# Start-up transfers reordered, two constant rows written on the chip, and two smaller expert buffers in a fused attention, gate and expert kernel

## The chip, the cores and the metric

The kernel runs on one core of a Trainium2 chip. The metric is the device time of one execution in microseconds (us); the number of record is the median of several executions. A profiled execution gives, beside its time, a trace of every instruction on the five engines: TensorE (PE, its weight loads apart as PEld), VectorE (DVE), ScalarE (ACT), GpSimd (POOL) and SyncE (SP, which here only issues transfers).

## The reference

Three layers follow each other on a batch of 2 sequences of 768 tokens. Attention has 8 heads of 64; a query sees the keys that fall to the same of 16 centroids. A gated projection of width 512 follows, and then 8 experts of 512 x 1024 x 512, of which each token uses one.

```python
q_assign = np.argmax(np.einsum('bhsd,hcd->bhsc', q_n, c_n), axis=-1)
mask = q_assign[:, :, :, None] == k_assign[:, :, None, :]
scores = np.where(mask, scale * np.matmul(q, k.transpose(0, 1, 3, 2)), -1e9)
attn = softmax(scores); x = attn @ v
...
out = sigmoid(causal_conv5(x, conv_w)) * (x @ w_val) @ w_out
...
e = fresh_e if s == 0 or local_gate[b, s] < 0.5 else prev_e
h = np.maximum(x[b, s] @ w1[e], 0.0)
out[b, s] = p[e] * (h @ w2[e])
```

## The kernel before

Heads are taken in 8 pairs. For a pair, `load` (L155) brings the transposed queries `qt` and keys `kt`, 128 x 768 floats each, through SP's queue. `assign` (L165 to L211) finds the centroid of every token: PE multiplies `qt` and `kt` with the normalised centroids `cT` into `sim` (L172), DVE transposes that (L177), takes the maximum (L182), compares (L185) and transposes back (L188), and for the first pair L201 makes the one-hot rows `rb`. Those rows stand under the 64 rows of each head in `km` (keys) and `q2` (queries): rows 0 to 63 hold the rounded values, 64 to 79 the one-hot rows, 80 to 95 zeros, and row 96 of `km` ones, so that one product gives score, mask and maximum. `cT` is made by `setup` from `cw` (the centroids) and `ident` (an identity matrix), through DVE, ACT and one transpose on PE (L133 to L143). `fixed` fills rows 80 to 96 from an array of zeros and ones, called `one`, in main memory, with transfers that POOL issues; there are three sets of `km` and `q2` for the pairs to take in turn.

The order within the first pairs is written out by hand, as tables of places (`FIRST`, `ORDER`, `GO`, `PLAN`). An engine runs its instructions in the order in which the program issues them, and so DVE, in the first pair, transposes `sim` of the second pair (L177) ahead of making `rb` of the first (L201).

The experts are sorted by the number of their tokens. The one of rank r gets a buffer of `CAPS[r]` places, fixed when the program is built; up to 128 tokens of one expert are done ahead of the others. A token that finds no place is left to a loop at the end (`beyond`), which loads an expert's whole weights anew for a block of 128; its number of rounds is a value that the chip computes. The work on an expert is `up` (eight steps over the 512 inputs, L1408 and L1411, for buffers of 256 places or fewer) and `down` (L1447, and L1455 for a last tile of 32 or 64 tokens). In `up`, high and low part of the tokens stand side by side:

```python
nc.tensor.matmul(ps[:, m, :2 * n], lhsT=hi[:, k, ms], rhs=x[:, k, :2 * n], ...)   # L1408
nc.tensor.matmul(ps[:, m, :256], lhsT=lo[:, k, ms], rhs=x[:, k, :256], ...)       # L1411
```

with n the number of places: 2n columns in the first. In `down`, each full tile of 128 tokens, or of 96, takes three products of 512 columns for each of eight rows of weights (L1447). A last tile of 64 or 32 tokens takes plain 32-bit products in groups side by side instead (L1455), 256 columns wide for 64 tokens and 128 wide for 32:

```python
def rest(self, r):
    return m if (m := self.cap(r) % 128) in (32, 64) else 0
```

ACT and DVE round the weights (L1353, L1354) four to five steps ahead of PE.

Of the kernel before, what the change touches and what calls it, by code (L numbers as in the profile page):

```python
# [31 lines left out]
N = B * S  # L32


CAPS = [320, 288, 256, 224, 192, 192, 160, 128]
NC = 3
NBLK = 12
KEEP = -1.7881393e-07
# [1 line left out]
def tiles(n):  # L40
    return -(-n // 128)


def f32(ap):
    return ap.bitcast(F32)


class Attn:
# [41 lines left out]
    def consts(self):  # L90

        nc, g, cp, tp = self.nc, self.g, self.cp, self.tp
        self.cw = cp.tile([128, 128], F32, name="cw")
        nc.sync.dma_start(self.cw, g["cw"])
        nc.sync.dma_start(self.ident, g["ident"])
        self.before = cp.tile([128, 128], BF16, name="before")
        nc.gpsimd.dma_start(self.before, g["before"])

        self.oq = [cp.tile([128, S], F32R, name=f"oq{i}") for i in range(2)]
        self.eh = [cp.tile([128, 128], F32R, name=f"eh{i}") for i in range(2)]  # L100
        self.negbig = cp.tile([128, 1], F32, name="negbig")
        nc.vector.memset(self.negbig, -BIG)

    def fixed(self, i):

        nc, g = self.nc, self.g
        nc.gpsimd.dma_start(self.km[i][80:97, :, :].rearrange("o a s -> o (a s)"), g["one"])
        nc.gpsimd.dma_start(self.q2[i][80:96, :, :].rearrange("o a s -> o (a s)"), g["one"][0:16])

# [475 lines left out]
    def run(self, work, beside):  # L585

        G = B * NP
        drain = lambda it: [None for _ in it]
        self.tiles = [(gi, i, a) for gi in range(G) for i in range(0, 12, 1 if gi < 2 else 2)
                      for a in range(2 if gi < 2 else 3)]  # L590
        self.last = 0
        self.consts()
        self.step("one", 0)
        self.load(0)
        self.load(1)
        self.setup()
        self.first_pair(work)
        self.todo = [(gi, j) for gi in range(1, G) for j in range(NT)]
        for gi in range(1, G):
            self.pair(gi, work, beside)  # L600
        drain(work)
        self.pvs((G, 0))
        drain(self.sums_mm(G - 1))
        self.main.close()
# [664 lines left out]
class Ffn:  # L1269
# [16 lines left out]
    @staticmethod  # L1286
    def cap(r):
        return 128 if r < 0 else CAPS[r]

# [11 lines left out]
    def turn(self, ps, tag, pool, r, i):  # L1301

        nc, n = self.nc, self.cap(r)
        if i == 0:

            self.x[r] = pool.tile([128, KD, 2 * max(CAPS) if r >= 0 else n],
                                  F32R if r >= 0 else F32, tag="x", name=f"x{r}")
# [76 lines left out]
    def up(self, ps, pool, r, c):  # L1384
# [4 lines left out]
        if c == 0:  # L1389
            self.h[r] = [pool.tile([128, KF, max(CAPS)], F32R, tag=t, name=f"{t}{r}", bufs=1)  # L1390
                         for t in ("hh", "hl")]
# [93 lines left out]
    def run(self, wst, wp, pg, late, ctx):  # L1485
# [9 lines left out]
        def turn(r, i):  # L1495
            free = ("o2",) if tiles(CAPS[r - 1]) < 3 else ()
            spare = 0 < i <= len(free)
            self.turn(ps_o if spare else ps_t, free[i - 1] if spare else "t", p2, r, i)
# [3 lines left out]
        for s in range(8, last):  # L1502
            r, c = s // 8 - 1, s % 8
            if c == 4 and r + 2 < E:
                self.gather(pg, r + 2)
            if r + 1 < E and c >= 5 and c - 5 < tiles(CAPS[r + 1]):
                turn(r + 1, c - 5)
# [275 lines left out]
def consts():  # L1783
# [7 lines left out]
    e = np.arange(E, dtype=f)  # L1791
    cap = np.array(CAPS)
    i = np.arange(E)
# [43 lines left out]
def host_moe(inputs):  # L1837
    cc = np.ascontiguousarray
    o = {}

    o["w_val"], o["w_out"] = (cc(inputs["moe_" + n]).view(np.int64) for n in ("w_val", "w_out"))
    o["conv"] = cc(inputs["moe_conv_w"].T.reshape(KD, 128, KC).transpose(1, 0, 2)).view(np.int64)
    wgl = np.concatenate([inputs["moe2_w_gate"], inputs["moe2_w_local"]], axis=1)
    o["wgl"] = cc(wgl.reshape(KD, 128, E + 1).transpose(1, 0, 2))
    o["w1"], o["w2"] = cc(inputs["moe2_w1"]), cc(inputs["moe2_w2"])
    o["ident"] = np.eye(128, dtype=np.float32)
    o["rc"], o["tri"] = consts()
    o["jc"] = cc(np.repeat(np.arange(NBLK, dtype=np.float32)[:, None], 128, axis=1))
    return o
# [55 lines left out]
```

## Time and profile before

| | us |
|---|---|
| median of three runs (the others 560.71 and 567.31) | 566.21 |
| the profiled execution's own time | 563.89 |
| its span | 562.1 |
| PE busy | 522.1 |
| DVE busy | 387.3 |
| ACT busy | 293.8 |
| POOL busy | 257.9 |

Times in the rows are in us from the start of the span unless ns is written. A row of the timeline gives start, length, engine, line, operation, what is written and read, and in brackets how long the engine stood idle ahead of it and who ended that. PE's busy time includes the overlap of pipelined matmuls, so a busy PE isn't PE at its peak.

### The profile page before, as it was taken

What the parts mean: (1) busy time and instruction counts of PE and PEld (TensorE: products, weight loads), DVE (VectorE), ACT (ScalarE), POOL (GpSimd) and SP (SyncE); (2) the same over time, 40 slices, a digit from 0 to 9 for tenths busy, and PEclk for the clock granted to TensorE, in tenths of its full rate; (3) what the DMA queues carried; (4) which work ended last, traced back from release to release, by engine and by line L of the source; (5) the groups of instructions that cost most, each with busy time, mean ns of one, the idle gap of its engine ahead of it and who ended that gap; (6) DMA issues with size and microseconds to landing.
All of it is one profiled execution on the core that took longest, in us unless ns stands there. A gap on an engine that the chain in (4) does not pass through costs nothing. (4 is left out here: it accounts for less than half of the span.)

```text
span 562.1 us, 9334 instructions
## 1 busy us (share of the span) xinstructions
PE 522.1 (93%) x3328; PEld 387.0 (69%) x3328; DVE 387.3 (69%) x694; ACT 293.8 (52%) x569; POOL 257.9 (46%) x195
## 2 busy tenths in 40 slices
PE   3898979999998999999988999999999999999992
PEld 0564545565655665667678899859898888978892
DVE  4756768787788689767978563646737568479671
ACT  2635354554554565686464241435534548559671
POOL 4475728697897878877931010042013133022011
PEclk9998897999999999999999999999999999999997
DMA  8896284676757452200000038289364887556840
GB/s 203 216 228 184 88 219 127 172 185 169 199 153 174 120 141 81 67 12 0 1 10 0 21 108 305 94 272 342 114 205 162 281 251 232 179 182 211 295 166 14
DMA packets 53180, 86.90 MB, mean 155 GB/s; under 512 B 6313, under 2 KB 30321, under 8 KB 53132
## 3 DMA queue, kind: packets, MB, share of 16 engines
q1 hardware_dynamic: 49996, 78.36, 47.1%
q0 software_dynamic: 3136, 7.92, 4.4%
q8 instruction: 27, 0.44, 0.3%
q14 instruction: 21, 0.17, 0.1%
HBM read 59.65 MB, written 8.62 MB: 121 GB/s over the span
## 5 line engine op out<-in xcount | busy, mean ns | idle before, releaser
L307 DVE TENSOR_REDUCE mn<-mx 128x1 f32<-128x512 f32 (+1 forms) x156 | 94.3, 639 | 29.6 <-PE mx L303 29.4
L398 ACT ACTIVATE p<-s 128x384 f32<-128x384 f32 x168 | 75.4, 488 | 58.5 <-PE s L397 55.3
L1354 DVE TENSOR_TENSOR wl<-ws,wh 128x1024 fp32r<-128x1024 f32 x64 | 77.5, 1222 | 11.0 <-ACT wh L1353 9.8
L476 POOL TENSOR_TENSOR acc<-acc,p 128x768 f32<-128x768 f32 x42 | 84.4, 2033 | 0.5
L1353 ACT ACTIVATE wh<-ws 128x1024 fp32r<-128x1024 f32 x64 | 66.6, 1056 | 6.3 <-DMA ws<-in_w_dram 6.3
L396 PE MATMUL s<-xq,xk 128*128 128x384 f32 x168 | 63.9, 380 | 3.4 <-ACT p L398 3.4
L1480 POOL DMA_INDIRECT out_dram<-o,L x12 | 14.5, 1212 | 112.5 <-ACT o L1479 99.2
L492 PE MATMUL pv<-p,v 128*64 128x384 f32 x336 | 64.8, 507 | 0.0
L303 PE MATMUL mx<-km,q 80*128 80x512 f32 (+1 forms) x192 | 60.7, 387 | 2.3 <-DVE mn L307 1.9
L397 PE MATMUL s<-q,km 97*128 97x384 f32 x168 | 57.4, 342 | 0.0
L1408 PE MATMUL ph<-x,wh 128*128 128x384 f32 (+4 forms) x192 | 56.5, 338 | 0.0
L396 PEld LDWEIGHTS s<-xq,xk 128*128 128x128 f32 x168 | 32.0, 191 | 34.7 <-issue 19.2
L796 DVE SCALAR_TENSOR_TENSOR gp<-xT,cwt,gp 128x767 f32<-128x767 f32 (+3 forms) x32 | 51.5, 1625 | 2.5 <-ACT gp L790 2.1
L1411 PE MATMUL ph<-x,wl 128*128 128x256 f32 x192 | 51.6, 279 | 0.0
L303 PEld LDWEIGHTS mx<-km,q 80*128 80x128 f32 x192 | 37.3, 207 | 15.4 <-DVE mn L307 8.1
L492 PEld LDWEIGHTS pv<-p,v 128*64 128x64 f32 x336 | 20.7, 138 | 27.8 <-issue 27.4
L1447 PE MATMUL po<-wh,hh 128*128 128x512 f32 x96 | 39.0, 407 | 0.0
L1408 PEld LDWEIGHTS ph<-x,wh 128*128 128x128 f32 x192 | 36.1, 188 | 3.2 <-issue 1.0
L1447 PE MATMUL po<-wh,hl 128*128 128x512 f32 x96 | 37.8, 393 | 0.0
L1447 PE MATMUL po<-wl,hh 128*128 128x512 f32 x96 | 37.6, 391 | 0.0
L1411 PEld LDWEIGHTS ph<-x,wl 128*128 128x128 f32 x192 | 36.0, 188 | 0.1
L476 POOL TENSOR_TENSOR acc<-p,p 128x768 f32<-128x768 f32 x14 | 26.2, 1884 | 20.7 <-ACT p L398 20.7
(350 smaller groups left out, 1096.7 us busy)
## 6 DMA issues: line engine op xcount, KB each, us to landing
ws<-in_w_dram SPq DMA_DIRECT2D x72, 512.0 KB
qt<-in_qT_dram SPq DMA_DIRECT2D x8, 384.0 KB
kt<-in_kT_dram SPq DMA_DIRECT2D x8, 384.0 KB
q<-hiq SPq DMA_DIRECT2D x16, 192.0 KB
km<-hik SPq DMA_DIRECT2D x16, 192.0 KB
v<-in_v_dram SPq DMA_DIRECT2D x8, 384.0 KB
xk<-kt SPq DMA_DIRECT2D x16, 192.0 KB
xk<-hik SPq DMA_DIRECT2D x16, 192.0 KB
```

Of the source, the lines that this page charges most:

```text
L303: nc.tensor.matmul(ps[:, n * p:n * p + n], lhsT=q2[0:80, h, t * 128:t * 128 + 128], rhs=km[0:80, h, c:c + n], start=(p == 0), stop=True, s ...
L307: nc.vector.tensor_reduce(out=out, in_=src, axis=AX.X, op=ALU.max)
L396: nc.tensor.matmul(ps, lhsT=kl[:, h, ks], rhs=t1[:, h, hs], start=True, stop=False)
L397: nc.tensor.matmul(ps, lhsT=km[:97, h, ks], rhs=q2[:97, h, hs], start=False, stop=True)
L398: nc.scalar.activation(pt[:, h, hs], ps, AF.Exp, scale=1.0 / D ** 0.5)
L476: eng.tensor_tensor(t[:, h], p(0)[:, h] if first is None else t[:, h], p(j)[:, h], op=ALU.add)
L492: nc.tensor.matmul(self.pvt[64 * h:64 * h + 64, i, :HS], lhsT=v[:, j, 64 * h:64 * h + 64], rhs=pt[:, h, half(i)], start=False, stop=(j == ...
L1353: nc.scalar.activation(hi, t, AF.Copy)
L1354: nc.vector.tensor_tensor(lo, t, f32(hi), op=ALU.subtract)
L1408: nc.tensor.matmul(ps[:, m, :2 * n], lhsT=hi[:, k, ms], rhs=x[:, k, :2 * n], start=st, stop=False, skip_group_check=True)
L1411: nc.tensor.matmul(ps[:, m, :256], lhsT=lo[:, k, ms], rhs=x[:, k, :256], start=False, stop=sp, skip_group_check=True)
L1447: nc.tensor.matmul(self.po[r][i][:m], lhsT=a[:, k, ts], rhs=w[:, q], start=(k == 0 and z == 0), stop=(k == KF - 1 and z == 2))
```

## The change

There are three edits. The first pair's four transfers are issued ahead of everything else on SP, and those of `cw` and `ident` move from SP to ACT's queue. The rows of `km` and `q2` for the first pair are written by three memsets on POOL, from row 64 on, in place of two transfers of 17 and 16 rows of 1536 floats that POOL issued; the other pairs keep the transfers. The third and the sixth expert's buffers shrink from 256 to 224 and from 192 to 160 places.

```diff
-CAPS = [320, 288, 256, 224, 192, 192, 160, 128]
+CAPS = [320, 288, 224, 224, 192, 160, 160, 128]
...
-        nc.sync.dma_start(self.cw, g["cw"])
-        nc.sync.dma_start(self.ident, g["ident"])
+
+        nc.scalar.dma_start(self.cw, g["cw"])
+        nc.scalar.dma_start(self.ident, g["ident"])
...
     def fixed(self, i):
 
         nc, g = self.nc, self.g
+        if i == 0:
+
+            nc.gpsimd.memset(f32(self.km[0][64:96, :, :]), 0.0)
+            nc.gpsimd.memset(f32(self.km[0][96:97, :, :]), 1.0)
+            nc.gpsimd.memset(f32(self.q2[0][64:96, :, :]), 0.0)
+            return
...
         self.last = 0
+        self.load(0)
         self.consts()
         self.step("one", 0)
-        self.load(0)
         self.load(1)
```

The line numbers after the first edits are 7 higher. SP's queue at the start of the program, before (`qt_137`, `kt_139` are the first pair's, `qt_141`, `kt_143` the second's, `hiq` and `hik` their rounded values):

```order
L94 DMA cw<-in_cw_dram 128x128
L95 DMA ident<-in_ident_dram 128x128
L155 DMA qt_137<-in_qT_dram 128x768
L155 DMA kt_139<-in_kT_dram 128x768
L155 DMA qt_141<-in_qT_dram 128x768
L155 DMA kt_143<-in_kT_dram 128x768
L264 DMA q_0_85<-hiq_175 64x768 x2
L264 DMA km_88<-hik_194 64x768 x2
```

SP's queue at the same place with the change:

```order
L162 DMA qt_124<-in_qT_dram 128x768
L162 DMA kt_126<-in_kT_dram 128x768
L162 DMA qt_142<-in_qT_dram 128x768
L162 DMA kt_144<-in_kT_dram 128x768
L271 DMA q_0_85<-hiq_176 64x768 x2
L271 DMA km_88<-hik_195 64x768 x2
```

Two rows have left the head of SP's queue. ACT's first instructions with the change; before, they are the same without the two transfers:

```order
L95 DMA cw<-in_cw_dram 128x128
L96 DMA ident<-in_ident_dram 128x128
L142 ACT_TABLE_LOAD
L142 ACTIVATE css<-css 128x1
L268 ACTIVATE hiq_176<-qt_124 128x768
```

The two transfers stand ahead of ACT's first table load. PE at the end of the sixth expert and the start of the seventh, before (`po` are the outputs, `ws` the weights as loaded, `hr` the last tile's hidden values):

```order
L1447 MATMUL po_0_5589<-wh_5578,hl_5450 128x512
L1455 MATMUL po_1_5590<-ws_5380,hr_5476 64x256 x4
L1455 MATMUL po_1_5590<-ws_5400,hr_5476 64x256 x4
L1455 MATMUL po_1_5590<-ws_5419,hr_5476 64x256 x4
L1455 MATMUL po_1_5590<-ws_5447,hr_5476 64x256 x4
L1408 MATMUL ph_0_5672<-x_5603,wh_5597 128x320
```

PE at the same place with the change:

```order
L1454 MATMUL po_0_5590<-wh_5579,hl_5451 128x512
L1462 MATMUL po_1_5591<-ws_5381,hr_5477 32x128 x8
L1462 MATMUL po_1_5591<-ws_5401,hr_5477 32x128 x8
L1462 MATMUL po_1_5591<-ws_5420,hr_5477 32x128 x8
L1462 MATMUL po_1_5591<-ws_5448,hr_5477 32x128 x8
L1415 MATMUL ph_0_5689<-x_5604,wh_5598 128x320
```

Nothing has moved there: 16 products of 256 columns have become 32 of 128. In the same way the 32 first products of the third expert's `up` go from 512 to 448 columns and those of the sixth's from 384 to 320.

## Rows read from the trace of the kernel before

**Rows 1.** Stretches of 20 us: busy time and instructions of each engine, granted clock, transfers.

```profile
core 0: us, PE busy (x) PEld busy (x) DVE busy (x) ACT busy (x) POOL busy (x), PEclk, DMA share, GB/s
0.00:20.00 20.00, 9.01 (x57) 3.18 (x57) 10.35 (x24) 7.06 (x12) 9.59 (x19) 1.00 0.91 227
...
440.00:460.00 20.00, 20.00 (x106) 16.92 (x105) 16.86 (x27) 14.55 (x21) 6.07 (x5) 1.00 0.84 276
```

**Rows 2.** Waits from 437.8 to 552 us: sum, number, longest.

```profile
ACT hs L1416 <- PE ph L1411: 34.5, 9, 7.9
```

**Rows 3.** Stretches of single steps of four experts, the same columns as rows 1.

```profile
437.84:449.25 11.41, 11.41 (x69) 9.92 (x65) 6.76 (x12) 7.37 (x12) 1.37 (x1) 1.00 0.86 283
461.06:471.30 10.24, 10.24 (x65) 9.74 (x64) 5.90 (x8) 7.01 (x11) 1.35 (x1) 1.00 0.66 200
503.00:512.28 9.28, 9.28 (x66) 9.28 (x65) 5.07 (x8) 6.33 (x13) 1.15 (x1) 1.00 1.04 350
522.52:531.06 8.54, 8.54 (x67) 8.54 (x65) 4.53 (x7) 5.89 (x12) 1.18 (x1) 1.00 1.05 355
518.92:522.52 3.60, 3.60 (x33) 2.22 (x32) 2.50 (x4) 0.53 (x1) 0.00 (x0) 1.00 0.90 318
537.12:539.00 1.88, 1.88 (x65) 1.68 (x64) 1.88 (x3) 0.91 (x1) 0.00 (x0) 1.00 0.79 288
449.25:461.06 11.81, 11.81 (x59) 9.73 (x58) 10.09 (x16) 7.18 (x10) 4.70 (x4) 1.00 0.78 252
471.30:483.46 12.16, 12.16 (x58) 9.03 (x57) 9.02 (x11) 6.75 (x10) 3.39 (x3) 1.00 0.92 292
```

**Rows 4.** Timeline of SP at the start.

```profile
0.73 0.41 SPq L94 DMA_DIRECT2D cw<-in_cw_dram  x1
...
1.67 0.42 SPq L155 DMA_DIRECT2D qt<-in_qT_dram  x1
```

**Rows 5.** Timeline of PE at the start: first and last product with `cT`.

```profile
6.71 0.87 PE L172 MATMUL sim<-qt,cT 128*32 128x192 f32 x8 [2.00 <-DMA qt<-in_qT_dram]
...
11.84 0.87 PE L172 MATMUL sim<-kt,cT 128*32 128x192 f32 x8 [0.49 <-DMA kt<-in_kT_dram]
```

**Rows 6.** Timeline of DVE at the start.

```profile
2.63 0.29 DVE L133 TENSOR_TENSOR csq<-cw 128x128 f32<-128x128 f32 x1 [1.77 <-DMA cw<-in_cw_dram]
...
4.75 0.29 DVE L143 COPY cT<-pc 128x128 f32<-128x128 f32 x1 [0.57 <-PE pc L141]
...
9.53 0.58 DVE L177 STREAM_TRANSPOSE s<-sim 128x384 f32<-128x384 f32 x1 [4.22 <-PE sim L172]
...
11.89 0.58 DVE L188 STREAM_TRANSPOSE et<-eq 128x384 bf16<-128x384 bf16 x1
12.78 0.58 DVE L177 STREAM_TRANSPOSE s<-sim 128x384 f32<-128x384 f32 x1 [0.31 <-PE sim L172]
```

**Rows 7.** Stretch from 4 to 12 us, the same columns as rows 1.

```profile
4.00:8.00 4.00, 1.34 (x9) 0.41 (x9) 0.74 (x4) 0.84 (x1) 0.00 (x0) 1.00 1.09 294
8.00:12.00 4.00, 1.89 (x20) 0.56 (x24) 2.37 (x4) 0.84 (x1) 2.36 (x2) 1.00 1.02 242
```

**Rows 8.** Timeline of ACT at the start.

```profile
0.72 1.28 ACT L135 ACT_TABLE_LOAD   x1 [0.72 <-PEq L1894]
3.27 0.20 ACT L135 ACTIVATE css<-css 128x1 f32<-128x1 f32 x1 [1.27 <-DVE css L134]
```

**Rows 9.** Timeline of POOL at the start.

```profile
1.27 0.72 POOL L97 DMA_DIRECT2D before<-in_before_dram  x1 [0.84 <-POOLq L1894]
...
9.64 1.81 POOL L269 TENSOR_TENSOR kt<-kt,hik 128x768 f32<-128x768 f32 x1 [6.53 <-PE sim L172]
...
16.08 1.41 POOL L124 MEMSET oq<- 64x768 f32 x2
```

**Rows 10.** Stretch from 55 to 60 us, columns as rows 1; PE's idle time ahead.

```profile
55.00:60.00 5.00, 5.00 (x14) 2.48 (x12) 4.83 (x11) 1.07 (x3) 1.18 (x1) 0.50 0.42 120
52.26 0.52 PE L343 MATMUL mt<-identr,mfr 128*128 128x128 f32 x3 [2.19 <-DVE mfr L338]
```

## Prediction

> **What bounds the kernel now.** I read the stretches first. In the experts' part PE is busy for 20.00 of 20 us, while DVE, the next, is busy for 16.86 in its fullest stretch [rows 1]. PE runs its products one behind the other there, so what shortens a product shortens the end. The sum of waits says that the others are ahead: ACT stood idle nine times, 34.5 us in all, until PE had finished a step of `up` [rows 2]. The first 20 us are another matter. PE is busy for 9.01 of them and the transfers take a share of 0.91 [rows 1], so the timelines of the start have to be followed from wait to wait. The page's chain of waits doesn't help, since it ends within the last few microseconds.
>
> At the start PE begins its first product with `cT` at 6.71, when `qt` has landed, and its last at 11.84, when the second pair's `kt` has landed [rows 5]. DVE transposes the first result at 9.53 and has the first pair's one-hot form at 11.89 + 0.58 = 12.47. Then it waits 0.31 for the last `sim` and transposes it at 12.78 [rows 6]. The first pair's `rb` stands behind that on DVE, and with it the first products of the masked scores. So of the four transfers it is the last that sets the start's end; `cT`, ready at 4.75 + 0.29 = 5.04 [rows 6], doesn't.
>
> **The change part by part. The third expert.** Its `up` was 32 products of 512 columns and 32 of 256, and took 11.41 us. With 224 places it is what the fourth expert is now, 448 and 256 columns, which took 10.24 [rows 3]: 1.17 off. Its `down` keeps two tiles with three products each per row of weights, since 96 isn't 32 or 64. It took 11.81, and the fourth's, with a last tile of 96, 12.16 [rows 3]. The 0.35 between them also holds other turned tiles and starts, so the loss lies between 0 and 0.35; I take 0.2.
>
> **The sixth expert.** `up` goes from 9.28 to what the seventh shows, 8.54: 0.74 off. Its last tile goes from 64 to 32 tokens, from 3.60 to 1.88 [rows 3]: 1.72 off, the largest single term. The full tile stays. Smaller transposes, evictions and gathers are put at nothing: they lie on ACT, DVE and POOL beside PE, and if their cover went, the ACT waits [rows 2] would have to be used up first, 34.5 us over nine waits, some 3.8 each against 2.5 us that leave the sixth expert. On the path this sums to -1.17 + 0.2 - 0.74 - 1.72 = -3.43, with bounds of -3.2 and -3.7.
>
> **The transfers at the start.** `qt` is issued at 1.67 and now would be at 0.73, in the place of `cw` [rows 4]: 0.94 earlier, and the three others with it. The rows of zeros and ones leave the queues: 33 rows of 6144 bytes, 203 KB, which at the 294 and 242 GB/s of the stretch from 4 to 12 us [rows 7] are 0.7 to 0.8 us of transfer time ahead of the last `kt`. If both count in full, the last `kt` lands 1.7 earlier. But `cw` and `ident`, 64 KB each, now run among the four instead of ahead of them, and 131 KB at the same rates are 0.5 us. If they push the four back by all of that, 1.2 remains; if the transfers, full as they are [rows 7], gain by bytes alone, 0.75; and the trace doesn't show how two queues share, so a lower end of 0.3 is kept. The upper end is 2.2, if 6144 bytes into single rows cost twice their bytes' share. I take 1.4, between the two sums. The stages behind are tied to each other by waits, so a shift at the start should reach the end unchanged.
>
> DMA issue is the subject of a rule. SP's rows show that a transfer takes about 0.42 of the issuing engine [rows 4]. The Trainium skill, "DMA: Bandwidth & Descriptors", section "Issuing engines are not separate DMA queues", says that transfers run on the same 16 engines and interleave whoever issues them, and that a second issuer saves only issue time. By that rule the start's gain would be the bytes' 0.75 and the whole change 4.2 us. The stretch from 4 to 12 us, with its engines full [rows 7], agrees; the first microseconds, in which `qt` waits to be issued, don't.
>
> **ACT.** Two issues of 0.42 come ahead of its table load, which started at 0.72 and takes 1.28: it would end at about 2.9. The next instruction starts at 3.27, behind DVE [rows 8]. So this costs nothing while DVE isn't earlier, and at most 0.8 if it were; what is queued behind it, the rounding of `qt`, isn't on the path before `qt` lands.
>
> **POOL.** Its issue of `before` ends at 1.99, and the three memsets follow. None of 1536 columns is in the trace. Two of 768 columns took 1.41 [rows 9], so one of 1536 costs 1.4, and three 4.2: POOL is free at about 6.2. If partitions and columns both count against it, 3 x 2.8 puts that at 10.4. Its next work starts at 9.64 behind PE's second product [rows 9], with the change some 1.4 earlier, at 8.2. At 6.2 the memsets are hidden; at 10.4 they push POOL's subtraction of `kt` by 2.2, which only feeds a transfer for the lower scores, and those come after the first masked maxima. I take nothing. ACT's and DVE's writes of the one-hot rows now also wait for POOL, and come behind `rb`, so later than 12.
>
> **The sum.** -3.43 - 1.4 = -4.8 us. The profiled execution took 563.89, 562.1 of it the span; that less 4.8 is 559.1. The median of the three runs, 566.21, lies 2.3 above it, and the mean of the four executions is 564.5. I take that mean as the base: **560 us** rounded, 1.1% below the median.
>
> **The rivals. The start gives nothing.** Another late arrival takes the place of the last `kt`, for instance the rounded keys, whose transfers stand behind all four in SP's queue. For it: transfers are at 1.09 and 1.02 of their engines from 4 to 12 us [rows 7]. Against it: bytes leave this stretch. Only the experts' part remains: 564.5 - 3.4 = 561.
>
> **The constants come too late: slower.** `cw` was first in line and was there by 2.63; `cT` was ready 2.41 later, and from there two products of 0.87 and DVE's work from 9.53 to 12.47 lead to the transpose of the second pair [rows 5, 6]. That is 2.41 + 1.74 + 2.94 = 7.1 from `cw` to a point that stands at 12.78 now. So `cw` may land up to 5.7 and cost nothing beside today's start, and from 9.2 on it eats the experts' 3.4 too. If ACT's queue is served behind SP's, `cw` lands when the last `kt` does now, 11.84: the point moves to 18.9, 6.1 later, and the time is 564.5 + 6.1 - 3.4 = 567. For it: SP issues first and asks for 1.6 MB. Against it: POOL's `before`, issued at 1.27 on a third queue [rows 9], was in time. The same skill page, "Queues, rings and completion order", has each transfer engine take turns between queues, which would put `cw` behind about one of the four; no row here shows such turns.
>
> **A low-clock stretch goes.** From 55 to 60 us the granted clock is 0.50, the lower level of 1.2 GHz, after PE had stood idle for 2.19 us behind DVE [rows 10]. If the shift shortens that idle time and the clock stays at 2.4, up to half of these 5.0 busy us come back: 560 - 2.5 = 557. Against it: that idle time comes from DVE's order of work, which the change leaves alone.
>
> **It doesn't do what it says.** If the third expert had more than 224 tokens, or the sixth more than 160, the end's loop would run a round. From the 225th token on that costs 4.2 MB of weights, 15 us at 276 GB/s [rows 1], and two layers of products behind it; 15 more is an estimate from that: about 590. The reference's own inputs put 220 and 104 tokens there, so four places are left.
>
> **How the numbers follow.** The forecast has 0.70, no gain at the start 0.15, a low-clock stretch gone 0.08, constants too late 0.05, the extra round 0.02. Two per cent, 11.3 us, is about what a measurement of this kernel can tell from no change; the three runs lie 6.6 apart. The bounds of the terms give -3.5 to -5.9, so 558.6 to 561 around the base, and the runs' spread around their mean (-4 and +3) goes on top: **555.5 to 565**. That takes in the first three cases, and leaves out the other two and the far ends. Faster by over 2% needs less than 554.9, which takes the gone stretch and a low run: 0.05. Slower by over 2% is the extra round: 0.02. The rest, 0.93, is within 2%.
>
> **What would show it.** The first `sim` should start between 5 and 6.5, the last at about 10.4, and DVE's transpose of it at about 11.4. POOL's memsets should end by 7. `up` of the third and sixth expert should take 10.2 and 8.5, the sixth's last tile 1.9, and PE should still have no wait there. The prediction is wrong if PE waits in the sixth expert for rounded weights, if `cT` comes after 7.5, or if what the start gains is waited away before 60 us.

## The result: 1% faster, as forecast, but the start gained in another way

| | before | after |
|---|---|---|
| median of 20 runs each, us | 564.87 | 558.79 |
| lowest and highest | 560.71, 567.82 | 555.92, 564.18 |
| ratio, 95% interval | | 0.9905, 0.9883 to 0.9926 |
| span of the profiled execution | 562.1 | 558.3 |
| first product of the masked scores (`mx`) starts at | 16.11 | 14.98 |
| PE's work on the experts takes | 171.38 | 167.90 |

The forecast was 560 and no change that a measurement can tell at 2%; the ratio is 5.4 us off the time before. Ratios here leave out the runs of the slower state, over 1.5% above their kernel's fastest, and of the profiles below only that of "`cw` first, again" is from such a run. The experts first. These are stretches of the changed kernel, with the columns of [rows 1]: `up` and `down` of the third expert, `up` and the last tile of the sixth.

```profile
437.88:448.23 10.35, 10.35 (x68) 9.86 (x65) 5.92 (x12) 6.68 (x11) 1.35 (x1) 1.00 0.91 303
448.23:460.17 11.94, 11.94 (x58) 9.09 (x57) 10.32 (x17) 7.31 (x10) 4.45 (x4) 1.00 0.80 252
502.13:510.66 8.53, 8.53 (x66) 8.53 (x65) 4.53 (x7) 5.89 (x12) 1.18 (x1) 1.00 1.01 336
517.30:519.18 1.88, 1.88 (x65) 1.68 (x64) 1.88 (x4) 0.50 (x1) 0.87 (x1) 1.00 0.86 272
```

Beside [rows 3] that is 11.41 to 10.35, 11.81 to 11.94, 9.28 to 8.53 and 3.60 to 1.88: -1.06 + 0.13 - 0.75 - 1.72 = -3.40. PE is busy in all of each stretch, and ACT still waits for it, 32.4 us in eight waits where [rows 2] have 34.5 in nine:

```profile
ACT hs L1423 <- PE ph L1418: 32.4, 8, 7.8
```

The start is another matter. PE, DVE and POOL in the changed kernel, with the lines that answer to [rows 5, 6, 9] (line numbers 7 higher; the first two rows are PE's first and last product with `cT`, the third is the first `mx`):

```profile
7.24 0.87 PE L179 MATMUL sim<-qt,cT 128*32 128x192 f32 x8 [0.38 <-DVE cT L150]
...
9.16 0.87 PE L179 MATMUL sim<-kt,cT 128*32 128x192 f32 x8
...
14.98 1.01 PE L310 MATMUL mx<-km,q 80*128 80x384 f32 x2
```

```profile
4.43 0.29 DVE L140 TENSOR_TENSOR csq<-cw 128x128 f32<-128x128 f32 x1 [3.57 <-DMA cw<-in_cw_dram]
...
5.70 0.62 DVE L146 TENSOR_SCALAR cn<-cw,css 128x128 f32<-128x128 f32 x1
6.89 0.29 DVE L150 COPY cT<-pc 128x128 f32<-128x128 f32 x1 [0.56 <-PE pc L148]
8.81 0.58 DVE L184 STREAM_TRANSPOSE s<-sim 128x384 f32<-128x384 f32 x1 [1.36 <-PE sim L179]
...
11.78 0.54 DVE L184 STREAM_TRANSPOSE s<-sim 128x384 f32<-128x384 f32 x1
```

```profile
2.03 1.37 POOL L110 MEMSET km<- 32x1536 f32 x1
3.46 1.37 POOL L111 MEMSET km<- 1x1536 f32 x1
4.87 1.37 POOL L112 MEMSET q<- 32x1536 f32 x1
```

The first product now starts behind `cT`, not behind `qt`, and the last has no wait for `kt` any more. In the records of the transfers the last `kt` landed at 8.29, 3.5 earlier than the 11.80 before; the sum had allowed at most 2.2. And `cw` landed at 4.41 where it was 2.60, so `cT` was ready at 6.89 + 0.29 = 7.18 in place of 5.04. All four products ran behind it in one go, and from the first transpose at 8.81 to the second at 11.78 DVE had no gap. The transpose of the second pair went from 12.78 to 11.78 and the first `mx` from 16.11 to 14.98: 1.13 where the sum had 1.4.

### The profile page after: what moved, and what is told of

Its sections match the earlier page's. It is cut to its first block, busy times and chain, and to the rows that moved or that the text cites. A ratio compares the mean times of both kernels' runs of the same rounds, so it can differ in the third digit from the quotient of the medians.

```text
span 558.3 us, 9403 instructions
## 1 busy us (share of the span) xinstructions
PE 518.1 (93%) x3360; PEld 386.0 (69%) x3360; DVE 386.1 (69%) x694; ACT 292.1 (52%) x569; POOL 262.9 (47%) x196
## 5 line engine op out<-in xcount | busy, mean ns | idle before, releaser
L1415 PE MATMUL ph<-x,wh 128*128 128x448 f32 (+3 forms) x192 | 54.7, 329 | 0.0
L803 DVE SCALAR_TENSOR_TENSOR gp<-xT,cwt,gp 128x767 f32<-128x767 f32 (+3 forms) x32 | 49.8, 1571 | 2.5 <-ACT gp L797 2.1
```

## The experiments

Diffs are against the changed kernel where nothing else is said. "First `mx`" is the start of the first product of the masked scores, the end of the stretch in question. The ratios are to the kernel before, run beside each. The landings come from the transfers' records; the last `kt` is that of the second pair.

| kernel | buffers | `cw` lands | last `kt` lands | first `mx` | ratio, 95% interval |
|---|---|---|---|---|---|
| before | old | 2.60 | 11.80 | 16.11 | 1 |
| changed | new | 4.41 | 8.29 | 14.98 | 0.9905 (0.9883 to 0.9926) |
| changed, again | new | 4.56 | 8.65 | 14.98 | 0.9916 (0.9878 to 0.9955) |
| buffers only | new | 2.77 | 11.48 | 15.79 | 0.9981 (0.9945 to 1.0018) |
| buffers only, again | new | 2.78 | 12.08 | 16.39 | 0.9932 (0.9894 to 0.9970) |
| start only | old | 4.63 | 8.59 | 15.14 | 0.9993 (0.9960 to 1.0025) |
| memsets only | old | 2.79 | 8.68 | 13.91 | 0.9963 (0.9931 to 0.9995) |
| memsets, and bytes in 128 rows | old | 2.55 | 9.98 | 14.38 | 0.9984 (0.9948 to 1.0019) |
| without the memsets | new | 4.49 | 12.17 | 16.48 | 0.9891 (0.9850 to 0.9933) |
| without the new order | new | 2.78 | 8.78 | 14.15 | 0.9884 (0.9820 to 0.9948) |
| `cw` first | new | 2.96 | 9.25 | 13.72 | 0.9879 (0.9841 to 0.9916) |
| `cw` first, again | new | 3.00 | 8.88 | 13.72 | 0.9865 (0.9819 to 0.9912) |
| `cw` first, early memsets | new | 2.97 | 9.02 | 13.39 | 0.9895 (0.9857 to 0.9933) |
| `cw` last | new | 7.90 | 7.71 | 18.29 | 0.9934 (0.9907 to 0.9961) |

The kernel before and the two with buffers only have the same start: there the last `kt` scatters by 0.6 us and the first `mx` too.

### The two halves of the change

**Buffers only** (the kernel before with one line of the change):

```diff
-CAPS = [320, 288, 256, 224, 192, 192, 160, 128]
+CAPS = [320, 288, 224, 224, 192, 160, 160, 128]
```

> The kernel before with the two smaller buffers alone; the start is as before. Both theories expect the same here, and this run sets the size of the experts' term by itself: in the profile of the changed kernel the last product of the experts' part came 3.33 us earlier after a start of that part 0.15 later, so 3.5 us should leave the experts' part. If the two halves of the change simply add, the time is 3.4 to 3.5 us below the kernel before, a ratio of about 0.994, and the start's part is then the rest of 5.4 us, about 2. If the ratio comes out near 0.990, the start gave nothing at the end and what the profile of the changed kernel shows at the start is waited away; that is the rival.

**Start only** (the changed kernel with the old `CAPS`):

> The changed kernel with the old buffers of 256 and 192 places: the start's part alone. Theory: the first masked maximum came 1.1 us earlier and that shift reaches the end, so the time is 1 to 2 us below the kernel before, ratio 0.996 to 0.998, and with the experts' part alone it adds up to the whole change. Rival: the shift is taken up in the middle, where the clock's low stretches fall differently from execution to execution; then the ratio is 1.000 within its interval.

Neither ratio is decided by itself: both intervals hold 1, and the first lies above the 0.994 expected. The profiles are clearer. From the first `up` behind the tokens done ahead to the last `down` PE takes this, in the kernel before, with the buffers only, and with the start only, each from its own trace:

```profile
380.75:552.13 171.38, 171.38 (x1144) 148.44 (x1144) 114.68 (x157) 102.09 (x167) 33.85 (x28) 1.00 0.64 212
```

```profile
380.24:548.06 167.82, 167.82 (x1176) 146.40 (x1176) 113.31 (x157) 100.89 (x168) 33.40 (x28) 1.00 0.67 217
```

```profile
382.31:553.57 171.26, 171.26 (x1144) 148.34 (x1144) 114.60 (x157) 102.06 (x167) 34.68 (x28) 1.00 0.65 211
```

Over all profiled executions the four with the old buffers lie between 171.26 and 171.38, the ten with the new ones between 167.80 and 168.08. So the experts' term is 3.4 us without scatter. What scatters is the middle: from the first `mx` to the start of that stretch thirteen of the fourteen take from 363 to 370 us, whatever the kernel. The granted clock sorts them. In some executions it falls once more between 172 and 184 us; here are the kernel before, without it, and the changed kernel:

```profile
174.00:178.00 4.00, 3.14 (x17) 1.89 (x17) 3.54 (x6) 1.11 (x4) 4.00 (x4) 1.00 0.85 225
```

```profile
174.00:178.00 4.00, 3.73 (x11) 1.37 (x11) 3.20 (x6) 0.66 (x3) 4.00 (x4) 0.57 0.90 219
```

The five of the thirteen with such a stretch take 365.9 to 370.3 us for the middle, the eight without it 362.8 to 365.4; the fourteenth has one and another at 193, and takes 373.8. A start that is 1 us earlier drowns in that in any one execution. So I repeated the first:

> The smaller buffers alone, again: the first measure gave 0.9981 with an interval of 0.9945 to 1.0018, while the order and buffers without the memsets, whose start is no earlier than before, gave 0.9891. Theory: both are one true value of about 0.994, the experts' 3.45 us, seen through runs that scatter by 2 us. Rival: 0.998 holds, and the experts' part is worth less in the timed runs than in the profiled one.

It gave 0.9932, which holds 0.994 and speaks for the theory.

### Which part of the start gains

**Memsets only** (against the kernel before, in `fixed`; order and buffers as before):

```diff
+        if i == 0:
+            nc.gpsimd.memset(f32(self.km[0][64:96, :, :]), 0.0)
+            nc.gpsimd.memset(f32(self.km[0][96:97, :, :]), 1.0)
+            nc.gpsimd.memset(f32(self.q2[0][64:96, :, :]), 0.0)
+            return
```

> The kernel before with one edit of the change alone: the memsets on POOL in place of the two transfers of zeros and ones for the first pair; order and buffers as before. In the kernel before the last kt landed at 11.80 us, in the changed one at 8.29, 3.5 earlier. Theory: the two transfers, 17 and 16 rows of 6144 bytes, held the engines for much more than their bytes; without them the last kt lands at about 9.5, the other 1.2 coming from the earlier issue. As cT then stands at about 5, the second pair's transpose should come at about 10.5 to 11 and the time 1 to 2 us below before. Rival: they cost only their bytes, 0.7 to 0.8 us, the last kt lands at about 11, and most of the 3.5 comes from the order of issue; then the time is within 0.8 us of before.

It did more for the start than the whole change: the last `kt` landed at 8.68, and the first `mx` came at 13.91. So the memsets are the gain, and the two transfers cost the last `kt` about 3 us, not their bytes' 0.8. PE in this kernel:

```profile
5.82 0.87 PE L177 MATMUL sim<-qt,cT 128*32 128x192 f32 x8 [0.39 <-DVE cT L148]
...
8.73 0.87 PE L177 MATMUL sim<-kt,cT 128*32 128x192 f32 x8 [0.23 <-DMA kt<-in_kT_dram]
...
13.91 1.01 PE L308 MATMUL mx<-km,q 80*128 80x384 f32 x2
```

**Without the memsets** (new order and buffers, the two transfers kept; the diff is the one above taken out again):

> The change without its memsets: the new order and the smaller buffers, with the two transfers of zeros and ones kept. Theory: these two transfers are what held the four up, so the last kt lands at about 11, some 0.9 before its 11.80, which is the earlier issue alone; cw lands at 4.4 and cT stands near 7 as in the changed kernel, but the last kt sets the second pair's transpose again, at about 12; the first masked maximum comes at about 15.2, and the time is that of the experts' part and 1 us more, about 4.4 below before, ratio 0.992. Rival: the order alone brings the transfers forward, the last kt lands by 9.5, and the start is that of the changed kernel.

The last `kt` landed at 12.17, no earlier than with the start of before (11.48 to 12.08). The rival fell: the order alone brings it nothing, not even the 0.9 of the earlier issue that the theory had left it. PE waits 2.03 for it:

```profile
6.99 0.87 PE L173 MATMUL sim<-qt,cT 128*32 128x192 f32 x8 [0.38 <-DVE cT L144]
...
9.32 0.87 PE L173 MATMUL sim<-qt,cT 128*32 128x192 f32 x8 [0.82 <-DMA qt<-in_qT_dram]
12.21 0.87 PE L173 MATMUL sim<-kt,cT 128*32 128x192 f32 x8 [2.03 <-DMA kt<-in_kT_dram]
```

Its ratio, 0.9891, is as good as that of the changed kernel all the same, with a first `mx` 1.5 later. With a start no earlier than before, the experts alone give 0.994, just outside its interval. I take that as scatter, and say below what all ratios give together.

**Without the new order** (`cw` and `ident` first on SP, as before; memsets and new buffers stay):

```diff
-        nc.scalar.dma_start(self.cw, g["cw"])
-        nc.scalar.dma_start(self.ident, g["ident"])
+        nc.sync.dma_start(self.cw, g["cw"])
+        nc.sync.dma_start(self.ident, g["ident"])
...
-        self.load(0)
         self.consts()
         self.step("one", 0)
+        self.load(0)
```

> The change without its edit of the order: memsets and smaller buffers, with cw and ident first on SP as before. The run with the memsets alone had its first masked maximum at 13.91 us, the changed kernel at 14.98, the kernel before at 16.11. Theory: the order is a loss of 1.1 us at the start, since cw lands later on ACT's queue, and it reaches the end; so this kernel is about 1 us faster than the changed one, that is 6 to 7 us below before, ratio 0.988 to 0.989. Rival: what a start gains or loses is taken up by waits further on; then it stands level with the changed kernel, 0.990 to 0.991.

The first `mx` came at 14.15, 0.8 before the changed kernel's. At the start the new order is a loss; with the old buffers it is 15.14 (start only) against 13.91 (memsets only), 1.2. The ratio, 0.9884 from six runs, has both theories in its interval.

**`cw` first** (on SP ahead of the four, `ident` on ACT):

```diff
-        nc.scalar.dma_start(self.cw, g["cw"])
+        nc.sync.dma_start(self.cw, g["cw"])
         nc.scalar.dma_start(self.ident, g["ident"])
...
-        self.load(0)
         self.consts()
+        self.load(0)
         self.step("one", 0)
```

> The changed kernel with one transfer moved: the centroids (cw) are issued first on SP's queue again, ahead of the four of the two pairs, while ident stays on ACT and the memsets stay on POOL. Theory: in the changed kernel cw, alone on ACT's queue beside the four on SP's, landed at 4.41 us instead of 2.60, so that cT came at 7.18 and all four products with cT ran behind it; the last kt, landed at 8.29, no longer sets anything. With cw first it should land by about 2.6 again, cT stand at about 5, the first product start with qt at about 5.3, and the second pair's transpose at about 10.3 instead of 11.78; the time is 1 to 1.5 us below the changed kernel. Rival: the last kt still sets the transpose of the second pair, as the prediction argued; then cw's place changes nothing, or costs 0.4 us, the length of one issue.

> The version with cw first on SP, ident on ACT and the memsets on POOL, again: its first measure gave 0.9879. Its first masked maximum came at 13.72 us, 2.4 before that of the kernel before and 5.3 before what the version with cw last should show. Theory: ratio 0.988 to 0.990, 3.5 of the experts and 2.4 of the start, and 5 us below the version with cw last. Rival: no lower than the changed kernel's 0.9905, since the middle takes the start's further gain up.

`cw` landed at 2.96 and the second pair's transpose stood at 10.37, as the theory had it, with the first `mx` at 13.72; only the first product came later than expected, at 5.83, behind `cT`. The rival, that the last `kt` sets this transpose, fell: `kt` landed a microsecond later than in the changed kernel and the transpose came 1.4 earlier. The ratios 0.9879 and 0.9865 lie below the changed kernel's 0.9905 and 0.9916, but the intervals overlap; the distance to the version with `cw` last, measured beside the second, is 3.9 us where 5 were expected. That this version is faster by its 1.3 us is shown at the start and likely at the end, not settled.

### What the two transfers did

The transfers in the stretch from 6 to 8 us, with the columns of [rows 1] (last the transfers' share and GB/s): the kernel before, memsets only, and without the memsets.

```profile
6.00:8.00 2.00, 0.87 (x8) 0.23 (x8) 0.00 (x0) 0.84 (x1) 0.00 (x0) 1.00 1.11 238
```

```profile
6.00:8.00 2.00, 1.90 (x24) 0.43 (x20) 0.79 (x3) 1.35 (x2) 0.43 (x2) 1.00 0.96 378
```

```profile
6.00:8.00 2.00, 1.48 (x17) 0.78 (x17) 0.64 (x4) 0.94 (x2) 0.00 (x0) 1.00 1.15 238
```

The engines are full in all three, but with the two transfers among them they move 238 GB/s in place of 378. I had read the full share as a limit and 294 and 242 GB/s as the rate that goes with it [rows 7]. For the first, from 4 to 8 us, it was the disturbance: the memsets alone have 385 there. From 8 to 12 us they have 233 as well, when copies on the chip follow in SP's queue. To tell the form of these transfers from their amount and queue, **bytes in 128 rows** was run (against memsets only):

```diff
         if i == 0:
+            one = g["one"].rearrange("r c -> (r c)").rearrange("(p c) -> p c", p=128)
+            nc.gpsimd.dma_start(self.km[1][:, 0, 0:204], one)
+            nc.gpsimd.dma_start(self.q2[1][:, 0, 0:192], one[:, 0:192])
             nc.gpsimd.memset(f32(self.km[0][64:96, :, :]), 0.0)
```

> The kernel with the memsets alone, and beside them two transfers that POOL issues where the two of zeros and ones stood: nearly the same bytes from the same array, 104 and 98 KB, but into 128 rows of 816 and 768 bytes of the second pair's buffers, where later transfers overwrite them, in place of 17 and 16 rows of 6144. So the amount, the queue and the moment are kept, and the form alone is changed. Last kt: 11.80 us in the kernel before, 8.68 with the memsets alone. Theory: the few long rows are what costs; then the last kt lands at 9.2 to 9.5, its 8.68 and 0.5 to 0.8 for the bytes, and the first masked maximum stays within 0.5 of 13.91. Rival: any 200 KB of a second queue beside SP's costs the 3 us; then the last kt lands at 11 or later, and the first masked maximum stands near 16.

The same stretch, and PE's last product with `cT` and first `mx`:

```profile
6.00:8.00 2.00, 1.61 (x16) 0.27 (x15) 0.08 (x2) 1.44 (x2) 1.40 (x1) 1.00 1.14 398
```

```profile
10.03 0.87 PE L180 MATMUL sim<-kt,cT 128*32 128x192 f32 x8 [0.91 <-DMA kt<-in_kT_dram]
...
14.38 1.01 PE L311 MATMUL mx<-km,q 80*128 80x384 f32 x2
```

The last `kt` landed at 9.98, between the two expectations and nearer to the theory's 9.2 to 9.5 than to the rival's 11. Of the 3.1 us between 8.68 and 11.80, 1.3 go with the bytes and 1.8 with the form, or 1.5 to 2.1 with the scatter of that start. The records of single packets show where most of it lies: a row of `qt` or `kt` is a packet of 3072 bytes and takes 121 to 126 ns on average from 5 to 8 us with the memsets alone. In the kernel before, the 33 packets of 6144 bytes took 352 ns each and beside them, from 5 to 9 us, the 3072-byte packets took 168 to 254 on average. Beside the bytes in 128 rows they took 126 to 133 from 5 to 8 us. The 33 long packets are 11.6 us of engine time, 0.7 of all 16, as the bytes had it; the other packets' slowness, some 275 of them by about 90 ns, is 1.5 more; the other 0.9 of the 3.1 I can't place. So beside the few long rows the loads' packets are slow, and beside the same bytes in 128 rows hardly. That run changed the number of rows and the length of a packet together, so which of them counts is open. The Trainium skill, "SBUF — State Buffer", section "Door 1: The DMA port swizzle", says that transfers reach the memory through 16 ports, and that a transfer into few rows reaches few of them. By its table rows 80 to 95 lie on four. The estimate from its 436 GB/s for all 16 is 1.8 us of those four ports for 32 rows, against 0.5 if all shared them: 1.3 too much, beside 1.8 measured. The size comes near; no run here wrote the rows over other ports, so that it is the ports isn't shown.

### What `cw` and the memsets do to `cT`

**`cw` last** (`cw` and `ident` on SP behind all four transfers):

```diff
-        nc.scalar.dma_start(self.cw, g["cw"])
-        nc.scalar.dma_start(self.ident, g["ident"])
+        nc.sync.dma_start(self.cw, g["cw"])
+        nc.sync.dma_start(self.ident, g["ident"])
...
         self.load(0)
+        self.load(1)
         self.consts()
         self.step("one", 0)
-        self.load(1)
```

> The changed kernel with cw and ident on SP behind all four transfers of queries and keys: a larger dose of the lateness of cw, to see whether a shift at the start reaches the end. The second pair's transpose came 7.35 us after cw landed in the changed kernel. Here cw should land at 8.3 to 8.8 us, with the memsets on POOL over by then, so that transpose should stand at about 15.7 instead of 11.78 and the first masked maximum at about 19 instead of 14.98. Theory: the shift of 4 reaches the end, so the time is about 563, level with the kernel with the experts' part alone or a little above, ratio 0.996 to 0.999. Rival: the middle has slack that takes such shifts up; then the time stays near 559 to 560, ratio 0.990.

DVE in this kernel:

```profile
7.92 0.29 DVE L139 TENSOR_TENSOR csq<-cw 128x128 f32<-128x128 f32 x1 [7.06 <-DMA cw<-in_cw_dram]
...
9.19 0.29 DVE L145 TENSOR_SCALAR cn<-cw,css 128x128 f32<-128x128 f32 x1
...
14.94 0.54 DVE L183 STREAM_TRANSPOSE s<-sim 128x384 f32<-128x384 f32 x1
```

From 7.90 to 14.94 are 7.04, beside the 7.1 of the prediction and 4.41 to 11.78 = 7.37 in the changed kernel; the 0.33 between are `cn`, 0.62 there and 0.29 here, where POOL's memsets are over. All four products wait for `cT` here, and the first `mx` came at 18.29, 3.3 after the changed kernel's. The ratio rose to 0.9934, between the rival's 0.990 and the theory's 0.996 to 0.999. Its interval just holds the theory's lower edge, leaves out the rival's by little, and overlaps with the changed kernel's. Against the changed kernel's 0.9905 it is 1.6 us for a first `mx` 3.3 later; against `cw` first, again, measured beside it, 3.9 for 4.6. So a part of the shift came through, and how much this run alone doesn't tell.

**`cw` first, early memsets** (against `cw` first):

```diff
-        nc.gpsimd.dma_start(self.before, g["before"])
...
             nc.gpsimd.memset(f32(self.km[0][64:96, :, :]), 0.0)
-            nc.gpsimd.memset(f32(self.km[0][96:97, :, :]), 1.0)
+            nc.vector.memset(f32(self.km[0][96:97, :, :]), 1.0)
             nc.gpsimd.memset(f32(self.q2[0][64:96, :, :]), 0.0)
+            nc.gpsimd.dma_start(self.before, g["before"])
```

> The version with cw first on SP and ident on ACT, and two edits more: the memsets stand ahead of POOL's issue of the matrix 'before', and the row of ones is written by DVE, which is idle there. In the runs with cw first, DVE's cn took 0.66 to 0.82 us beside a memset on POOL, against 0.29 in the kernel before. Theory: the two slow each other; with POOL's memsets over by about 3.5, cn takes 0.29 again and cT stands 0.4 earlier, at about 5.4 us. Since the first kt lands at about 6.3, at most 0.2 of that reach the first transpose: about 7.2, and the first masked maximum at about 13.5. The time is level with the other version with cw first, 7 to 8 us below before, ratio about 0.987. Rival: cn is slow for another reason, the transfers then running, and stays at 0.6 or more.

DVE and POOL in this kernel:

```profile
1.22 1.34 DVE L109 MEMSET km<- 1x1536 f32 x1 [0.36 <-issue]
...
4.26 0.29 DVE L145 TENSOR_SCALAR cn<-cw,css 128x128 f32<-128x128 f32 x1
5.12 0.29 DVE L149 COPY cT<-pc 128x128 f32<-128x128 f32 x1 [0.57 <-PE pc L147]
```

```profile
0.72 1.37 POOL L108 MEMSET km<- 32x1536 f32 x1 [0.29 <-POOLq L1900]
2.04 1.37 POOL L110 MEMSET q<- 32x1536 f32 x1
```

`cn` takes 0.29 again, with the loads still running beside it: the theory held. The first `mx` came at 13.39, the earliest of all. The ratio, 0.9895, is level with the others with new buffers; its interval holds the 0.987 expected too.

### Does the start reach the end?

The changed kernel was run again as a measure for the runs beside it:

> The changed kernel again, as the measure for the three others on the same chip. Both theories: ratio 0.9905 as measured, within 0.003.

It gave 0.9916. One ratio tells a shift of 1 us poorly, the thirteen of the table together do better. A least-squares fit of (ratio - 1) x 564.9 us, weighted by the intervals, to one value for the new buffers and one for each us of first `mx` against 16.11 gives -4.5 +- 0.3 us for the buffers and 0.67 +- 0.17 us for each us (one standard error). The ratios lie 1.3 times as far from the fit as their intervals say, so 0.4 and 0.2 are the safer errors; the runs of before are also shared between kernels of one group. So a shift of the start reaches the end in the main; that nothing of it does lies three such errors off, and that all of it does 1.5. For the changed kernel the fit gives -4.5 - 0.67 x 1.13 = -5.3, where the ratio gives -5.4. That the buffers come out at 4.5, and at 3.4 in every trace, is 1 us which I can't place; it is some two and a half of its errors. Without `cw` last the same fit gives -4.1 and 0.88, with errors of 0.6 and 0.3.

The traces say the same for the executions without the further low stretch between 172 and 184 us. Four of them have a start without memsets (first `mx` at 15.79 to 16.48, the mean 16.2) and come to the first `up` behind the tokens done ahead at 380.3 on average, the other four (13.72 to 14.98, 14.2) at 378.1: 2.1 us for 2.0. But that stretch is in none of the four executions without memsets and in six of the ten with them. Whether another start brings it on these runs don't tell; if it does, it takes a part of the gain back.

## Why the prediction was right

**The experts' part** was right in every term: -3.40 in the stretches for -3.43, no term off by more than 0.11. PE had no wait there, and the smaller evictions and gathers cost nothing, as said.

**The start** had a size that was near, 1.1 for 1.4, by luck, and a mechanism that was wrong. The step that failed is "So of the four transfers it is the last that sets the start's end; `cT`, ready at 4.75 + 0.29 = 5.04, doesn't". That was true of the kernel before, and the change ended it. Two errors stood against each other. The transfers of zeros and ones were priced by their bytes, with twice that as the upper end; they were worth 3.1 us of the last `kt`. And the other half of the change, the order, was credited with up to 0.94; it cost 0.8 to 1.3, the first `mx` at 14.98 with it against 14.15 and 13.72 with `cw` first. (In the start only, with the same transpose at 11.78, the first `mx` stands at 15.14; the 0.16 between are the clock of the last section.) The rival "the constants come too late" described the place rightly: its 7.1 us from `cw` to the transpose held within 0.3, and `cw` at 4.41 kept the bound of 5.7 for being no slower than before. ACT's queue wasn't served behind SP's: `cw` came ahead of the first `qt`, which landed at 5.03. I used the 7.1 only for the loss, not as the next limit of the gain: with the measured 4.41 it gives 11.5, later than the 11.4 that the last `kt` was to allow.

**POOL and ACT.** Memsets of 1.4 each that end at 6.2 were right (1.37, 6.24), also that one row costs what 32 do. That they cost nothing was not quite: in the changed kernel `cn` starts at 5.70 and ends at 6.32, 0.08 after the third memset's 6.24. With the memsets alone it ends 0.08 after the second. In the three executions with the changed kernel's start `cw` landed at 4.41, 4.56 and 4.63, and `cn` ended at 6.32 and the first product began at 7.24 in all of them: what `cT` waited for last was the third memset. The Trainium skill, "SBUF — State Buffer", section "SBUF: two separate sides", says that DVE and POOL share a pair of ports under a lock that one holds for a whole instruction; both ends and the 0.29 without a memset agree. ACT's two issues were hidden, since its next step waited for DVE until 5.08.

**The signs.** `up` at 10.2 and 8.5, the last tile at 1.9 and the memsets' end by 7 were met. The first product came at 7.24 instead of 5 to 6.5, the last at 9.16 instead of 10.4, and the transpose at 11.78 instead of 11.4. `cT` came at 7.18, inside the bound of 7.5 that was to show a wrong start, and set the start all the same. What the start gains wasn't waited away before 60 us: in both profiled executions of the changed kernel it was gone at 53 us, by the clock and not by a wait, and 0.8 of it was back at 60, as the last section shows. In the run with the start alone 1.0 was there at 54 us and 0.7 at 60. **The low-clock stretch** around 55 us [rows 10] stayed, from 51.5 to 58.3, and no extra round ran.

**Two of the bounds** don't follow from their terms. For the start's upper end 0.94 and twice the bytes' 0.75 are 2.4, and 1.9 less the 0.5 of `cw` and `ident`, not 2.2; and 558.6 to 561 with -4 and +3 on top is 554.6 to 564, not 555.5 to 565. The measured 558.79 lies in either.

## What to carry to other kernels

A transfer of a few long rows can cost far more than its bytes, here four times: look at what the other packets take beside it, and if the content is a constant, write it on the chip. When a change removes the wait that ended last, ask at once which of the others is next, and hold the whole change against that one: here a small constant at the head of a chain of 7 us was worth its place ahead of 1.5 MB of bulk. Move one part at a time; here the better half hid the loss of the other, and both looked like one gain of the expected size.

## What the runs showed of the hardware

The granted clock after the four products that run in one go. Two stretches of the changed kernel, then the stretch from 32.76 to 34.40 of the kernel before, of the changed kernel and of the start only:

```profile
10.51:13.92 3.41, 0.67 (x9) 0.19 (x8) 3.31 (x7) 0.06 (x1) 2.88 (x3) 1.00 0.97 236
13.92:34.40 20.48, 18.30 (x59) 13.47 (x60) 14.39 (x30) 12.66 (x26) 11.81 (x21) 0.50 0.79 197
```

```profile
32.76:34.40 1.64, 1.63 (x8) 0.84 (x6) 1.64 (x4) 0.66 (x2) 1.56 (x4) 1.00 1.07 207
```

```profile
32.76:34.40 1.64, 1.64 (x6) 0.78 (x5) 0.88 (x2) 0.49 (x1) 1.64 (x4) 0.50 0.98 177
```

```profile
32.76:34.40 1.64, 1.64 (x7) 0.58 (x6) 1.05 (x3) 0.49 (x1) 1.64 (x4) 1.00 1.02 182
```

In both profiled executions of the changed kernel the clock stood at 2.4 GHz from 10.5 to 13.9 us, just after the products in one go from 7.24 to 10.03, and PE stood idle for 1.89 us before its next product, at 11.91. It fell to 1.2 and came back at 34.4, 1.6 later than in the kernel before. In the start only the same products stand at the same times, but there is no early rise on record, and the clock rose at 32.69 to stay; so the products alone don't make the difference. Of the start's 1.1 us the two executions have 0.3 to 0.4 left from 34.5 to 50 us, the start only 0.7 to 0.8. Then the low-clock stretch around 55 us begins and ends 1.8 us earlier than in the kernel before (51.47 to 58.29 against 53.24 to 60.06). The same two groups of products, first in the kernel before, then in the changed kernel:

```profile
52.85 1.20 PE L303 MATMUL mx<-km,q 80*128 80x384 f32 x3
...
60.14 1.26 PE L441 MATMUL pv<-p,v 128*64 128x384 f32 x4
```

```profile
52.95 1.16 PE L310 MATMUL mx<-km,q 80*128 80x384 f32 x3
...
59.35 1.40 PE L448 MATMUL pv<-p,v 128*64 128x384 f32 x4
```

At 53 us, with the changed kernel at 1.2 GHz and the kernel before still at 2.4, nothing is left; behind both low stretches 0.8 is there again. The column reads 1.00 ahead of 32.76 in the kernel before, but the first `mx` took 1.01 us there as in the changed kernel at 0.50, so a 1.00 ahead of the first rise on record says nothing. Over the timed runs an execution with an early rise shows by a mean clock below 0.967: 11 of 32 of the changed kernel, 4 of 12 with the start only, 4 of 11 with `cw` last, 1 of 12 with early memsets, none of the others. Against the rest of the same runs their means are 1.2 us longer and, in the second series, 0.6 shorter for the changed kernel, 1.2 longer with the start only and 1.8 longer with `cw` last. So they are perhaps 1 us slower, which such a scatter doesn't settle.

A memset of 1536 columns took 1.37 to 1.43 us on POOL, over 32 rows or one, and 1.34 on DVE over one.
